# RWKV-5 attention into a cosine-routed mixture of experts: two experts named early, part of the first run as plain products

## The chip, the cores and the metric

One core of a Trainium2 chip runs the kernel. Its engines are PE (TensorE, matrix products), DVE (VectorE), ACT (ScalarE), POOL (GpSimd) and SP (SyncE, which issues DMAs here); PEld is PE's loading of weights. The metric is device time in microseconds (us), lower is better.

## The reference

```
for t in range(S):                      # B, H, S, D = 4, 8, 768, 48
    cur = einsum('bhd,bhe->bhde', u * k[t], v[t])
    y[t] = einsum('bhd,bhde->bhe', r[t], state + cur)
    state = w * state + einsum('bhd,bhe->bhde', k[t], v[t])
x = y as (B*S, H*D) = (3072, 384)
logits = (x / |x|) @ (emb / |emb|).T / tau       # 8 experts
idx = argmax(logits); gate = softmax(logits)[idx]
for e in range(8):                      # F = 1024
    h = relu(x[idx == e] @ w1[e])       # 384 -> 1024
    out[idx == e] = gate * (h @ w2[e])  # 1024 -> 384
```

## The kernel before

**Attention** runs in chunks of 64 steps, `attend` for each of 24 units (12 chunks, two units each); a unit is 128 rows of x. K, R and V are loaded chunk by chunk on SP's queue, four slots deep. ACT stores each chunk's rows to a scratch in DRAM, `xs` (L682 before, L684 after). **Routing** is done in four groups of 8, 8, 4 and 4 units (`route`): logits, the winner, its place in the expert's list by products with a triangle and with ones (L786, L787), and an addition to the list `L` (L843). It is a chain between DVE and PE.

**Settle** comes after the last group: the experts are sorted by load (`rank`, `sel`, `perm`) and `mine` takes out of `L`, for each run, the rows to gather and to write and their gates. Run i is the expert with the i-th largest load and is compiled for `CAPS[i]` rows; a row count above a cap sets a flag, and `again` does everything once more in a slow general way. `fetch` loads the weights of run i on SP (1.5 MB for w1, 1.5 MB for w2) into one of two buffers each.

**An expert** (`gather`, `expert`, `rest`): the rows of runs 0 and 1 are gathered from `xs` by POOL's indirect DMA and turned by PE (L982), those of the others by a way through DRAM and a DVE transpose. Layer one and the first 256 rows of layer two are Strassen-Winograd products with seven products for eight (L1092 and L1193); rows 256 to 383 of layer two are plain (L1170), rows from 384 on are `rest` (L1252). DVE makes the sums of w1 (L1035 to L1038), of w2 and of x (L1043 to L1046). A scatter by POOL writes the rows (L1155).

**The order** is not the program's. `Plan` records every operation with a guessed duration and its predecessors, and a list scheduler (`Plan.run`) puts out for each engine a fixed order: of the operations that can start within 0.1 us of the earliest one it takes the lowest `rank`, which is the number of the operation unless given. It also models one DMA pipe at 200 KB per us.

## Time and profile before

| | us |
|---|---|
| median of 3 runs | 451.37 (450.65 to 451.65) |
| the profiled execution | 448.21 |
| its span, first to last instruction | 446.0 |

| engine | busy us | share of the span |
|---|---|---|
| PE | 381.8 | 86% |
| PEld | 326.0 | 73% |
| DVE | 261.0 | 59% |
| POOL | 152.2 | 34% |
| ACT | 140.3 | 31% |

The busy share is a mean over three stages: attention (to about 147 us), the change-over (routing of the last group, settle, first gathers; to 182.84 us) and the experts (to the end). What the page and the trace say of each is in the rows below. Names such as `arena` are shared memory, so a line number says more than a name.

### The profile page before, as it was taken

Reading aid. Unit: us, or ns where it says so; the run is one execution under the profiler, and the core shown is the slowest. Engines: PE = TensorE matmul, PEld = TensorE weight load, DVE = VectorE, ACT = ScalarE, POOL = GpSimd, SP = SyncE. Lnnn points to the kernel's source line nnn. Section 1 sums busy time; section 2 is a strip of 40 time slices with the busy share of each in tenths; the row PEclk is TensorE's granted clock in tenths of the full one; section 3 lists DMA queues with packets and bytes.
Section 4 is the critical chain, followed back from the end, with each engine's and each line's share of the span. In section 5 each row is a group of like instructions: output and inputs, shape, how many; then the busy total and the mean of one; then the engine's idle time right before and its main releaser. Section 6 shows DMA issues by size and latency. Waiting matters only on the chain. (4 is left out here: it accounts for less than half of the span.)

```text
span 446.0 us, 11709 instructions
## 1 busy us (share of the span) xinstructions
PE 381.8 (86%) x4804; PEld 326.0 (73%) x4804; DVE 261.0 (59%) x563; ACT 140.3 (31%) x293; POOL 152.2 (34%) x188
## 2 busy tenths in 40 slices
PE   5888878988979512799999999999999999999993
PEld 3767757776758311685995896997997978979973
DVE  3885618775976388337266377377456564663521
ACT  1344523555344200032232332332141331322410
POOL 6869474866470133540160203230201201202001
PEclk8599988999898655699999999999999999999999
DMA  9766777867621169562474337346336352601001
GB/s 131 139 145 132 154 145 140 187 144 163 130 73 38 37 219 383 189 179 110 140 244 157 118 121 247 117 143 205 138 99 213 130 189 117 210 1 45 8 13 41
DMA packets 106678, 61.70 MB, mean 138 GB/s; under 512 B 87480, under 2 KB 101264, under 8 KB 106618
## 3 DMA queue, kind: packets, MB, share of 16 engines
q1 hardware_dynamic: 95770, 45.94, 38.5%
q0 software_dynamic: 3360, 9.44, 6.2%
q10 hardware_dynamic: 7488, 5.51, 4.1%
q8 instruction: 39, 0.64, 0.6%
q14 instruction: 21, 0.17, 0.1%
HBM read 48.43 MB, written 13.17 MB: 138 GB/s over the span
## 5 line engine op out<-in xcount | busy, mean ns | idle before, releaser
L1155 POOL DMA_INDIRECT out_dram<-arena,take x27 | 31.5, 1168 | 156.1 <-DVE arena L1044 70.0
L1092 PE MATMUL sc<-arena 128*128 128x192 f32 (+3 forms) x200 | 40.7, 337 | 1.1 <-ACT arena L1105 1.1
L1001 POOL DMA_INDIRECT G<-xs,take x19 | 20.6, 1086 | 54.4 <-DMA way<-G 39.9
L1092 PEld LDWEIGHTS sc<-arena 128*128 128x128 f32 x200 | 33.6, 190 | 4.2 <-ACT arena L1105 3.9
L1092 PE MATMUL yy<-arena 128*128 128x192 f32 (+3 forms) x176 | 35.4, 336 | 0.8 <-ACT arena L1105 0.6
L1116 ACT ACTIVATE arena<-arena 128x768 f32<-128x768 f32 (+3 forms) x32 | 27.5, 865 | 24.8 <-DVE arena L1109 23.9
L1092 PE MATMUL st<-arena 128*128 128x192 f32 (+3 forms) x168 | 34.5, 345 | 0.6 <-ACT arena L1105 0.6
L597 POOL TENSOR_TENSOR arena<-id,own 128x512 f32<-128x512 f32 x24 | 26.6, 1113 | 19.2 <-DVE own L593 15.9
L546 POOL TENSOR_TENSOR arena<-arena,kpow 128x384 f32<-128x384 f32 x24 | 24.6, 1024 | 21.6 <-PE tr L584 11.8
L1092 PEld LDWEIGHTS yy<-arena 128*128 128x128 f32 x176 | 29.7, 190 | 3.1 <-ACT arena L1105 2.3
L1092 PEld LDWEIGHTS st<-arena 128*128 128x128 f32 x168 | 29.6, 197 | 2.2 <-ACT arena L1105 1.6
L1092 PE MATMUL tr<-arena 128*128 128x192 f32 (+3 forms) x160 | 31.1, 331 | 0.0
L1092 PEld LDWEIGHTS tr<-arena 128*128 128x128 f32 x160 | 27.3, 190 | 0.3 <-ACT arena L1105 0.3
L1193 PE MATMUL yy<-arena 128*128 128x192 f32 x144 | 26.7, 330 | 0.9 <-ACT arena L1204 0.9
L590 POOL TENSOR_TENSOR arena<-arena,u_bc 128x384 f32<-128x384 f32 x24 | 25.0, 1044 | 6.9 <-DMA arena<-in_r_dram 6.6
L1193 PEld LDWEIGHTS yy<-arena 128*128 128x128 f32 x144 | 23.6, 190 | 2.9 <-ACT arena L1204 1.6
L1193 PE MATMUL st<-arena 128*128 128x192 f32 x120 | 22.4, 329 | 0.4 <-ACT arena L1204 0.4
L660 PE MATMUL st<-arena 64*64 64x48 f32 x704 | 18.1, 240 | 5.3 <-DMA arena<-in_v_dram 3.3
L660 PEld LDWEIGHTS st<-arena 64*64 64x64 f32 x704 | 15.0, 152 | 9.8 <-issue 4.3
L576 DVE TENSOR_TENSOR arena<-tr,pow 128x512 f32<-128x512 f32 x24 | 16.4, 685 | 9.1 <-PE tr L570 6.0
L1193 PEld LDWEIGHTS st<-arena 128*128 128x128 f32 x120 | 19.7, 190 | 1.8 <-ACT arena L1204 0.8
L591 DVE TENSOR_TENSOR arena<-arena 128x384 f32<-128x384 f32 x24 | 19.3, 803 | 2.2 <-POOL arena L590 2.1
(225 smaller groups left out, 767.6 us busy)
## 6 DMA issues: line engine op xcount, KB each, us to landing
arena<-in_moe_w_dram SPq DMA_DIRECT2D x10, 1536.0 KB
arena<-in_moe_w_dram SPq DMA_DIRECT2D x18, 512.0 KB
arena<-in_k_dram SPq DMA_DIRECT2D x48, 96.0 KB
xs<-arena ACTq DMA_DIRECT2D x12, 384.0 KB
arena<-in_r_dram SPq DMA_DIRECT2D x44, 96.0 KB
arena<-in_v_dram SPq DMA_DIRECT2D x44, 96.0 KB
Gq<-way SPq DMA_DIRECT2D x73, 48.0 KB
way<-G SPq DMA_DIRECT2D x18, 192.0 KB
```

Of the source, the lines that this page charges most:

```text
L546: p.op("POOL", gp(384), lambda: G.tensor_mul(Kw.t[:, :, 0:D], Ku(), kpow.t), r=[*Ks, kpow, k.pads], w=[Kw])
L576: lambda: V.tensor_mul(four(RT.t), four(rt.t), rpow.t[:, :, None, :].to_broadcast([128, NP, 2, C])),
L590: p.op("POOL", gp(384), lambda: G.tensor_mul(RU.t, Ru()[:, :, 0:D], k.u_bc.t), r=[*Rs, k.u_bc], w=[RU])
L591: p.op("DVE", 0.86, lambda: V.tensor_mul(RU.t, RU.t, Ku()), r=Ks, w=[RU])
L597: lambda: G.tensor_mul(AT.t, k.id64.t[:, None, None, :].to_broadcast([128, 2, NP, C]), own.t.rearrange("q (p s) -> q s p", s=2)[:, :, :, N ...
L660: mm(st.t[s * DP : (s + 1) * DP, b, (g * NP + q) * D : (g * NP + q + 1) * D], Kw.t[side(x), 2 * q + s, :], Vu()[side(x), 2 * q + s], start ...
L1001: lambda rows=rows, j=j: G.indirect_dma_start(out=rows.t[:, :], out_offset=None, in_=k.xs[:, :], in_offset=IndirectOffsetOnAxis(ap=k.take. ...
L1092: mm(bank.t[:, s * hn : (s + 1) * hn], left(2 * g + s), right(), start=(first and s == 0 and m == 0), stop=False, skip_group_check=True,)
L1116: lambda: A.activation(hT.t[:, 4 * a + 2 * g : 4 * a + 2 * g + 2, 0:n], hT.t[:, 4 * a + 2 * g : 4 * a + 2 * g + 2, 0:n], ACT.Relu),
L1155: now = G.indirect_dma_start(out=k.out[:, :], out_offset=IndirectOffsetOnAxis(ap=k.take.t[0:tn, i, 1, j : j + 1], axis=0), in_=y.t[0:tn, : ...
L1193: mm(bank.t[:, 0:192], left(s), right(s), start=(first and s == 0), stop=False, skip_group_check=True)
```

## The change

- `choose`, after the second routing group (16 of 24 units): the two experts with most rows so far are named (`two`, `perm2`), and the list of the first 256 rows of the fuller one is taken out (`take_e`, `gate_e`). `fetch` for runs 0 and 1 is recorded behind units 17 and 19 and reads `perm2`.
- `plainly`: those 256 rows (`EARLY`) go through both layers as plain products, relu and gate on ACT, with a rank of 20000 and more, so behind all else that can go; only their gathers keep a usual rank. After settle the remaining 176 rows of run 0's cap (432 - 256) go the same way, with rank 30000 and more. Run 0 has no Strassen products any more.
- `settle` does `mine` for runs 1 and 0 first; the others are sorted with a bonus that keeps the two named ones in front.
- `CAPS` goes from 432, 416, 400, 384 to 432, 416, 416, 400 for runs 0 to 3; the rest stay at 384.
- Routing operations behind the first three of a group get 60, 30, 40 and 0 added to their rank (`LATER`), except the two that free the PSUM bank.
- The shared memory of the experts is laid out anew.

```diff
+LATER = (60, 30, 40, 0)
-CAPS = (432, 416, 400, 384, 384, 384, 384, 384)
+CAPS = (432, 416, 416, 400, 384, 384, 384, 384)
+EARLY = 256
...
-        o.rank = len(self.ops) if rank is None else rank
+        o.rank = len(self.ops) + self.base if rank is None else rank
...
+    p.base = LATER[n]
     best = small("best", full)
...
+def choose(k):
...
+    def heaviest(i):
+        V.reduce_max(top.t[:, i : i + 1], so_far.t, axis=AX.X)
+        V.tensor_scalar(k.two.t[:, i], so_far.t, top.t[:, i : i + 1], None, ALU.is_equal)
...
+    p.op("DVE", 0.2, lambda: V.tensor_copy(k.perm2.t, permf.t), r=[permf], w=[k.perm2])
...
+    p.op("DVE", 0.25, lambda: V.reduce_sum(got.t, prod.t, axis=AX.X), r=[prod], w=[got])
+    p.op("DVE", 0.2, lambda: V.tensor_scalar_add(k.take_e.t, got.t[:, 1:3], float(SKIP)), r=[got], w=[k.take_e])
...
 def settle(k):
+    for i in (1, 0):
+        mine(k, i)
...
-    for i in range(E):
+    for i in range(2, E):
         mine(k, i)
...
+def plainly(k, weights, count, rows_of, gate, take, where, after):
...
+    for j, (t0, tn) in enumerate(parts(count)):
+        rows = Val(k.G, "G")
+        base, p.base = p.base, 0
+        p.op(
+            "POOL", 1.3,
+            lambda rows=rows, j=j: G.indirect_dma_start(
+                out=rows.t[:, :], out_offset=None, in_=k.xs[0:rows_of, :],
+                in_offset=IndirectOffsetOnAxis(ap=where(j, 0), axis=0),
+                bounds_check=rows_of - 1, oob_is_err=False,
+            ),
+            r=[take], w=[rows], done=2.5, kb=192, after=after,
+        )
+        p.base = base
...
+        p.op("PE", 0.36, turn, r=[rows, k.ident], w=[ps], mode=128)
...
+    for f in range(NF):
+        ps = Val(k.tre, "he")
+        def one(ps=ps, f=f):
+            for m in range(NK):
+                mm(
+                    ps.t[:, 0:count], w1.t[:, m, f * 128 : (f + 1) * 128], xT.t[:, m, 0:count],
+                    start=(m == 0), stop=(m == NK - 1),
+                )
+        p.op("PE", 3 * count * 0.00167, one, r=[w1, xT, *xs], w=[ps], mode=128)
...
+    for j, (t0, tn) in enumerate(parts(count)):
...
+        p.op("PE", 8 * 0.644 / q + 0.1, two, r=[w2, hT, *hs], w=[ps], mode=z)
...
+                if u_ + 1 == ends[1]:
+                    choose(n)
+                if u_ == 17:
+                    weights = [fetch(n, 0)]
+                if u_ == 19:
+                    weights.append(fetch(n, 1))
...
+            p.base = 20000
+            plainly(
+                n, weights[0], EARLY, 128 * ends[1], lambda j, tn: n.gate_e.t[0:tn, j : j + 1], n.take_e,
+                lambda j, a: n.take_e.t[:, a, j : j + 1], [n.stored],
+            )
+            p.base = 0
             settle(n)
-            weights = [fetch(n, i) for i in range(2)]
-            rows = [gather(n, 0)]
-            for i in range(E):
+            rows = [None, gather(n, 1)]
+            p.base = 30000
+            plainly(
+                n, weights.pop(0), CAPS[0] - EARLY, N, lambda j, tn: n.gate.t[0:tn, 0, EARLY // 128 + j : EARLY // 128 + j + 1],
+                n.takes[0], lambda j, a: n.take.t[:, 0, a, EARLY // 128 + j : EARLY // 128 + j + 1], [n.xsv.last],
+            )
+            rows.pop(0)
+            p.base = 40000
+            weights.append(fetch(n, 2))
+            for i in range(1, E):
```

**Place 1, PE, from the last routing group to the first expert.** Before: the list (L835), the total load (L856), then the turning of gathered rows (L982, buffers `G`) up to the first Strassen products.

```order
L835 MATMUL tr_69<-put_89,lanes_87 128x96 x4
L856 MATMUL tr_68<-pre_84,ones 128x8
L982 MATMUL st<-ident,G_93 128x128 x3
L1293 TENSOR_LOAD flag
L982 MATMUL st<-ident,G_94 128x128 x3
L982 MATMUL sc<-ident,G_95 128x128 x3
L982 MATMUL sc<-ident,G_96 128x48 x3
L982 MATMUL yy<-ident,G_93 128x128 x3
L982 MATMUL yy<-ident,G_94 128x128 x3
L982 MATMUL tr_69<-ident,G_95 128x128 x3
L982 MATMUL tr_68<-ident,G_96 128x32 x3
L1092 MATMUL st<-arena 128x216 x8
```

After: the total load is L937; L1352 turns gathered rows of `plainly`, L1371 is its layer one (eight groups of three), L1391 its layer two, L1064 turns the rows of run 1; the first five rows are:

```order
L937 MATMUL tr_69<-pre_84,ones 128x8
L1352 MATMUL tr_68<-ident,G_94 128x128 x3
L1371 MATMUL tr_69<-arena 128x256 x3
L1371 MATMUL tr_68<-arena 128x256 x3
L1371 MATMUL tr_69<-arena 128x256 x3
```

The products of the early rows stand behind the total load; after the sixth group of L1371, come:

```order
L1064 MATMUL st<-ident,G_95 128x128 x3
L1371 MATMUL tr_69<-arena 128x256 x3
L1064 MATMUL st<-ident,G_96 128x128 x3
L1371 MATMUL tr_68<-arena 128x256 x3
L1064 MATMUL sc<-ident,G_93 128x128 x3
L1064 MATMUL sc<-ident,G_94 128x32 x3
L1391 MATMUL tr_69<-arena 128x384 x8
L1467 TENSOR_LOAD flag
L1391 MATMUL tr_68<-arena 128x384 x8
```

The turning of run 1's rows stands between the groups of the early layer one, ahead of the early layer two.

**Place 2, ACT, the last stores to `xs`.** Before: the last store (L682) stands directly behind the copy of the last unit's result (L651).

```order
L700 COPY arena<-tr_68 128x384
L651 COPY arena<-yy 128x2x4x48
L682 DMA xs<-arena 128x2x384
L690 ACTIVATE arena,ssq<-arena 128x384
L700 COPY arena<-tr_69 128x384
L720 COPY ls_78<-tr_68 128x128
L791 ACTIVATE d_173<-d_173 128x32
L1293 TENSOR_LOAD flag
```

After: the copies of the units are L653, the squares L692, the exponential of the last routing group L794, the copies of turned early rows L1361, their relu L1380.

```order
L653 COPY arena<-yy 128x2x4x48
L692 ACTIVATE arena,ssq<-arena 128x384
L702 COPY arena<-tr_68 128x384
L722 COPY ls_78<-tr_69 128x128
L794 ACTIVATE d_184<-d_184 128x32
L684 DMA xs<-arena 128x2x384
L1361 COPY arena<-tr_68 128x3x128
L684 DMA xs<-arena 128x2x384
L1380 ACTIVATE arena<-tr_69 128x256
L1380 ACTIVATE arena<-tr_68 128x256
```

The last two stores (L684) now stand behind the exponential, and the last one behind the copy of the second early tile.

**Place 3, DVE, from the end of settle to the first copy of turned rows.** Before: the last reciprocal of `mine` (L921), the load check (L1282 to L1289), then the first copy (L991) ahead of the sums of w1.

```order
L921 RECIPROCAL gate<-gate 128x4
L1282 TENSOR_TENSOR loads<-sel,load 128x64
L1283 TENSOR_REDUCE sorted<-loads 128x8
L1285 TENSOR_SCALAR sorted<-sorted 128x1 x8
L1286 TENSOR_REDUCE over<-sorted 128x1
L1287 TENSOR_TENSOR over<-over,far 1x1
L1288 CAST flag<-over 1x1
L1289 CAST flag<-far 1x1
L991 COPY arena<-st 128x3x128
L1035 TENSOR_TENSOR arena<-arena 128x512
L1036 TENSOR_TENSOR arena<-arena 128x512
```

After: the last reciprocal of `mine` is L1003, the sums of w1 are L1119 and L1120 (L1117 and L1118 stand ahead of settle), those of w2 L1125 to L1128, the first copy of turned rows L1073.

```order
L1003 RECIPROCAL gate<-gate 128x4
L1119 TENSOR_TENSOR arena<-arena 128x512
L1120 TENSOR_TENSOR arena<-arena 128x512
L1125 TENSOR_TENSOR arena<-arena 128x768
L1126 TENSOR_TENSOR arena<-arena 128x768
L1127 TENSOR_TENSOR arena<-arena 128x768
L1128 TENSOR_TENSOR arena<-arena 128x768
L1073 COPY arena<-st 128x3x128
L1456 TENSOR_TENSOR loads<-sel,load 128x64
L1457 TENSOR_REDUCE sorted<-loads 128x8
```

The sums of w2 now stand ahead of the first copy.

## Rows read from the trace of the kernel before

**Rows 1.** The page's part 2: PE and its clock in 40 slices.

```profile
PE   5888878988979512799999999999999999999993
...
PEclk8599988999898655699999999999999999999999
```

**Rows 2.** Windows: busy PE, PEld, DVE, ACT, POOL; PEclk, DMA share, GB/s.

```profile
150.00:183.00 33.00, 9.37 (x40) 7.37 (x39) 24.73 (x97) 0.23 (x1) 10.79 (x10) 0.50 0.67 241
```

**Rows 3.** Timeline of PE in the change-over: start us, us, instruction [wait].

```profile
146.54 0.55 PE L696 MATMUL tr<-ident,arena 128*128 128x128 f32 x3 [0.60 <-ACT arena L651]
...
156.33 0.49 PE L856 MATMUL tr<-pre,ones 128*128 128x8 f32 x2
...
166.04 0.90 PE L982 MATMUL st<-ident,G 128*128 128x128 f32 x3 [9.22 <-DMA G<-xs,take]
...
182.84 3.92 PE L1092 MATMUL st<-arena 128*128 128x216 f32 x12
```

**Rows 4.** Timeline of PE, runs 0 to 4; last, an ACT copy (lines view).

```profile
188.20 1.62 PE L1092 MATMUL sc<-arena 128*128 128x216 f32 x8
...
189.69 1.00 PE L1092 MATMUL st<-arena 128*128 128x216 f32 x4
...
203.79 1.45 PE L1170 MATMUL st<-arena 128*128 128x384 f32 x4
...
209.68 2.79 PE L1252 MATMUL sc<-arena 128*48 128x384 f32 x16
...
212.39 1.57 PE L1193 MATMUL st<-arena 128*128 128x192 f32 x8
...
238.50 1.45 PE L1170 MATMUL tr<-arena 128*128 128x384 f32 x4
...
271.62 1.45 PE L1170 MATMUL tr<-arena 128*128 128x384 f32 x4
...
303.72 1.45 PE L1170 MATMUL st<-arena 128*128 128x384 f32 x4
...
333.46 1.45 PE L1170 MATMUL st<-arena 128*128 128x384 f32 x4
...
L700 ACT COPY arena<-tr 128x384 f32<-128x384 f32 x24 | 11.4, 477 | 9.4 <-PE tr L696 9.4
```

**Rows 5.** Windows as in group 2, finer.

```profile
130.00:135.00 5.00, 3.28 (x74) 2.51 (x75) 4.60 (x16) 1.31 (x4) 3.05 (x4) 0.96 0.00 0
...
135.00:140.00 5.00, 4.93 (x96) 4.34 (x91) 3.71 (x8) 2.15 (x5) 0.17 (x1) 0.70 0.01 3
...
184.00:186.00 2.00, 2.00 (x7) 1.88 (x7) 0.00 (x0) 0.00 (x0) 1.00 (x1) 0.54 0.40 144
```

**Rows 6.** Timeline of DVE between attention and the first expert.

```profile
156.58 0.25 DVE L843 TENSOR_TENSOR L<-L,tr 128x96 f32<-128x96 f32 x1 [2.12 <-PE tr L835]
...
166.42 0.18 DVE L921 RECIPROCAL gate<-gate 128x4 f32<-128x4 f32 x1
...
170.54 0.68 DVE L1038 TENSOR_TENSOR arena<-arena 128x512 f32<-128x512 f32 x1
...
175.26 0.95 DVE L1046 TENSOR_TENSOR arena<-arena 128x768 f32<-128x768 f32 x1
```

**Rows 7.** ACT's last store to xs; DMA tenths, 140 to 160 us.

```profile
146.52 0.38 ACTq L682 DMA_DIRECT2D xs<-arena  x1
...
DMA  0893100000000119910000000000000000000000
```

**Rows 8.** Gathers L971 and their landing; landing of the later ones, L1001.

```profile
L971 POOL DMA_INDIRECT G<-xs,take x8: 997/1006/1475, 159.5 to 178.0; - x8
...
DMA to landing us min/median/max: 4.3/6.0/6.8
...
DMA to landing us min/median/max: 3.0/5.9/7.4
```

**Rows 9.** Waits of PE, 45 to 147 us: total, times, longest.

```profile
PE tr L786 <- DVE oh L771: 2.8, 3, 1.1
```

More of the change, by code (lines that the diff above doesn't have):

```diff
@@ L852, in settle @@
     sb = lambda name, shape, dt=F32: p.fixed(k.sb(shape, name, dt), name)
+    k.take = sb("take", [128, E, 2, COLS], I32)
+    k.gate = sb("gate", [128, E, COLS])
+    k.got = sb("got", [128, E, 3, COLS])
+    k.gots = [p.fixed(None) for _ in range(E)]
+    k.takes = [p.fixed(None) for _ in range(E)]
+    k.gates = [p.fixed(None) for _ in range(E)]
     ct = Val(k.trr, "ct")
@@ L863, in settle @@
     )
+    for i in (1, 0):
+        mine(k, i)
+    ladj = sb("ladj", [128, E])
+    p.op(
+        "DVE", 0.21,
+        lambda: V.scalar_tensor_tensor(ladj.t, k.bonus.t, 65536.0, load_.t, ALU.mult, ALU.add), r=[k.bonus, load_], w=[ladj],
+    )
     gt = sb("gt", [128, E, E])
@@ L868, in settle @@
         lambda: V.tensor_tensor(
[L869 removed]
+            gt.t, ladj.t[:, None, :].to_broadcast(sq), ladj.t[:, :, None].to_broadcast(sq), ALU.is_gt
         ),
[L871 removed]
+        r=[ladj], w=[gt],
     )
@@ L892, in settle @@
     k.load = load_
-    k.take = sb("take", [128, E, 2, COLS], I32)
-    k.gate = sb("gate", [128, E, COLS])
-    k.got = sb("got", [128, E, 3, COLS])
-    k.gots = [p.fixed(None) for _ in range(E)]
-    k.takes = [p.fixed(None) for _ in range(E)]
-    k.gates = [p.fixed(None) for _ in range(E)]
-    for i in range(E):
+    for i in range(2, E):
         mine(k, i)
@@ L1153, in scatter @@
     def scatter(y, j, tn):
-        def put():
-            now = G.indirect_dma_start(
-                out=k.out[:, :], out_offset=IndirectOffsetOnAxis(ap=k.take.t[0:tn, i, 1, j : j + 1], axis=0),
-                in_=y.t[0:tn, :], in_offset=None, bounds_check=N - 1, oob_is_err=False,
-            )
-            for before in k.scatters:
-                k.tc.declare_no_dep(now.ins, before.ins, reason="each row of the output is in one list once")
-            k.scatters.append(now)
-        p.op("POOL", 1.3, put, r=[y, k.takes[i]], done=2.0, kb=192)
+        send(k, y, k.takes[i], lambda: k.take.t[0:tn, i, 1, j : j + 1], tn)
     gate = lambda j, tn=128: k.gate.t[0:tn, i, j : j + 1]
@@ L1236, in expert, with send, put @@
     blocks()
+def send(k, y, take, where, tn):
+    G = k.nc.gpsimd
+    def put():
+        now = G.indirect_dma_start(
+            out=k.out[:, :], out_offset=IndirectOffsetOnAxis(ap=where(), axis=0),
+            in_=y.t[0:tn, :], in_offset=None, bounds_check=N - 1, oob_is_err=False,
+        )
+        for before in k.scatters:
+            k.tc.declare_no_dep(now.ins, before.ins, reason="each row of the output is in one list once")
+        k.scatters.append(now)
+    k.plan.op("POOL", 1.3, put, r=[y, take], done=2.0, kb=192)
@@ L1470 @@
         cell = [object() for _ in range(10)]
-        n.tr, n.trx, n.trr = (p.pool(tr, [(cell[0],), (cell[1],)]) for _ in range(3))
+        n.tr, n.trx, n.trr, n.tre = (p.pool(tr, [(cell[0],), (cell[1],)]) for _ in range(4))
         n.Y = p.pool([sc, yy], [(cell[2], cell[3]), (cell[4], cell[5])])
```

128 lines of the change are left out of this document (117 added, 11 removed).

## The prediction

> **What bounds the kernel now.** I read the page's slices first. PE is at 9 in every slice from the eighteenth on and mostly at 8 in attention, but slices 14 to 17 read 5, 1, 2, 7, with PE's clock at 5 and 6 [rows 1]. Three stages then: attention, bound by PE and its partners together; a change-over in which PE has little to do; the experts, bound by PE. The windows give the hole its size: of the 33 us from 150 to 183, PE is busy 9.4, at half clock, while DVE is busy 24.7 and the DMA engines move 241 GB/s [rows 2]. The timeline says what fills it: the last product of a unit starts at 146.54, the total load ends at 156.82, the first gathered row is turned only at 166.04 after a wait of 9.22 us for its gather, and the first expert product starts at 182.84 [rows 3]. So about 26 us behind the total load are a wait for lists, gathers, 6.3 MB of weights and sums on DVE, and PE could do other work in them if it had rows and weights.
>
> **The sum** is made at one mark that both programs have: the start of the plain layer two products of run 1, at 238.50 [rows 4], L1243 in the changed kernel. Behind it the order is of the same kind; only the caps differ.
>
> Start. In the new order the early products stand directly behind the total load. I take its end as 156.82 here too (attention, below). Then come three turns of the second early tile, 0.90 at half clock [rows 3], its copy by ACT, 0.48 [rows 4], and two handoffs, 0.2 each as an estimate: layer one starts at 158.6.
>
> PE work from there. Four products of 216 columns take 189.69 - 188.20 = 1.49 us, so 1.72 ns a column [rows 4]. Early layer one: 24 x 256 columns, 10.6. Early layer two, two sets of the eight products that take 209.68 - 203.79 less a wait of 0.37, 5.5 each: 11.0. Late layer one: 24 x 176 columns, 7.3. Late layer two: one such set and 48 rows like L1252's, 212.39 - 209.68 = 2.7: 8.2. Layer one of run 1: from 212.39 to 238.50 are 26.1, of which 28 products of 192 columns take 9.2, leaving 16.9 with its own waits. Six tiles to turn, 0.45 each at full clock: 2.4, a little less for the narrow ones. Together 56.4.
>
> Losses. First the clock: from 182.84 on the products ran at 1.2 GHz, and the window from 184 to 186 still reads 0.54 [rows 5], so the rise came 3 us after the start; the same again costs 1.5. Second, a wait that the change adds. The turning of run 1's second tile writes the bank pair of the first and waits for DVE to copy it (L1073), and DVE now has the sums of w2 ahead of that copy. Behind the list at 156.58, settle took until 166.60 [rows 6]; with one operation more it ends at 166.8; two sums of w1 at 0.7 and four of w2 at 0.9 [rows 6] and the copy at 0.5 bring it to 172.2. PE gets there after six groups, one turning and a seventh: 158.6 + 1.5 + 7.9 + 0.45 + 1.3 = 169.8. Wait 2.4, and 0.6 more at the fourth tile, whose copies stand behind the load check: 3.0. In the queue behind it stands all the rest of PE's work. Third, the clock may fall in that wait: after the routing waits of the window from 130 to 135 it fell, and 135 to 140 reads 0.70 at 4.93 busy [rows 5], which is 3 us at half clock, 1.5 lost. From 0 to 1.5, I take 0.7. Fourth, the flag load that now stands between the early layer two sets, and the relu behind each layer's end: 0.4 each as at L1170, 0.8. Together 6.0, bounds 2.5 to 9.
>
> The mark falls at 158.6 + 56.4 + 6.0 = 221.0, which is 17.5 earlier.
>
> Caps. From mark to mark of the next runs are 33.1, 32.1 and 29.7 [rows 4], for caps 416 then 400, 400 then 384, 384 and 384. Runs 2 and 3 now have 416 and 400, so 33.7 (44 x 8 columns more), 33.1 and 32.1: 4.0 more. From the products alone it would be 2.6; I take 4.0, since the rows hold the handoffs too.
>
> Attention. Added to it are 16 small operations on DVE in `choose` at about 0.2 (the kind of L921) [rows 6] and two gathers on POOL at 1.0 to 1.5 [rows 8]; the next units' squares, masks and products with u queue behind them: up to 5. Taken away are routing chains ahead of unit work: PE waits 2.8 for the winner (L786) [rows 9], and 1.5 goes to the clock that falls there [rows 5]: up to 4. Both sides are of a size; I take 0, with -4 and +5 for the range.
>
> Transfers. The 6.3 MB go from the change-over to the stretch behind the last loads, where the DMA share is 0.00 and 0.01 [rows 5]: nothing, as long as the names are there. They hang on the second routing group, two groups ahead of the total load. If they came so late that w1 of run 1 landed behind 154, its first two sums (L1117, L1118), which stand ahead of the list's addition on DVE, would hold settle and the gathers by as much. The stores to xs are moved the other way. Before, the last was issued at 146.52 and its bytes moved until 149 [rows 7]; now it stands on ACT behind the copy of the second early tile, so at 158.5, and run 1's gathers cannot start before 161.5, against 159.5 before. The first lands 3.0 to 6.8 after its issue [rows 8], by 164.5 to 168.3, and PE wants it at 168.0: hidden by a hair. Here the Trainium skill speaks against the change: "DMA: Bandwidth & Descriptors", section "Issuing engines are not separate DMA queues", says that transfers from all issuing engines share the same DMA engines and interleave, so moved weights would slow what they meet. The landing times agree, 6.0 in the middle beside the weights and 3.0 at best [rows 8]; by it an early gather lands 3 us later, which changes no term, since the second early tile is turned only behind the total load.
>
> Sum: -17.5 + 4.0 + 0 = **-13.5**, so a span of 432.5. The profiled execution took 448.21, of which 446.0 is the span; it would take 434.7. The median of the runs shown, 451.37, is 3.2 above it, so 437.9.
>
> **Rivals.** *A slide*: attention or settle gets longer by 4 to 11 us, because `choose` holds DVE and POOL in units 17 to 23, or the rows of run 1 land late. For it: POOL and DVE are in order and their new rows stand amid unit work. Against it: DVE is busy 4.6 and PE 3.3 of 5 us in 130 to 135 [rows 5], so there is room. Centre +6: 444. *More*: the routing waits go (-4), DVE's copies come in time (-3.7 with the clock): 430. For it: the planner has the same chains in view. Against it: the sums stand ahead of the copy in the order. *Slower*: PE's clock stays at 1.2 GHz through the early products, which have pauses for two PSUM banks and for DVE. Its place is 158 to 182, its price 21.6 more less the 1.5 counted, so +20: -13.5 + 20 = +6.6, 458. It decides from the point where 15 us of the early work, counted at full clock, run at half. For it: all of 150 to 183 reads 0.50 although PE turned eight tiles there [rows 2]. Against it: once products came back to back at 182.84, it rose in 3 us [rows 3, 5]. The skill's "TensorE: Matmul & The Clock Gate", section "A second HAM failure mode: psum-queue depth-cycling", tells of a kernel whose short idle times between groups, as it goes round the PSUM banks, make the clock swing; by that rule 458 could come, but the Strassen groups also go round the banks, and the clock stays at 9 there [rows 1]. *It does not do what it says*: the second name may be wrong. On these inputs (counted from the reference) the two fullest experts have 272 and 271 rows after 16 units and 427 and 408 in the end, so they stay the fullest, by one row in their order; were they swapped, 427 would exceed the cap of 416, and `again` would add some thousand us.
>
> **How the numbers follow.** The forecast has 0.71, with a range of its own of 432 to 443.5 (losses and attention off by some 4 together). The slide has 0.14, of which 0.11 still ends faster and 0.03 within 0.2%; more gain 0.10; the clock 0.04, the wrong name 0.01. A measurement of this kernel can tell about 0.2% from no change, 0.9 us. Faster 0.71 + 0.11 + 0.10 = 0.92, same 0.03, slower 0.05. The range leaves out the slower cases, the worse half of the slide and the better part of more gain: 430.5 to 445.
>
> **What would show it.** In the changed profile: weights moving at 125 to 150 and the DMA share falling in 160 to 180; PE at 9 from about 158 on; PE's clock at 1.00 from about 162; a wait of PE at L1064 for DVE's L1073 near 170, some 3 us; the mark L1243 near 221; the three steps behind it 33.7, 33.1 and 32.1. The prediction is wrong if the last unit ends more than 4 us off 147, if PE waits for a gather at L1064, if L1117 waits for weights, or if the steps between the marks are those of before.

## The result, and the profile after

The changed kernel takes **457.77 us** (median of 4 runs, 456.82 to 458.70) beside 451.51 for the kernel before in the same measurement (median of 4, 450.65 to 458.28): a ratio of **1.0145**, 95% interval 1.0115 to 1.0175. Every ratio here leaves out executions more than 1.5% above the fastest of their kernel, and no median does; without the 458.28 the kernel before has 451.37, so the change costs 6.4 us. The forecast was 437.9, range 430.5 to 445.0. The profiled execution took 456.82, its span is 455.0.

The page's slices of the changed kernel (PE, its clock, the DMA engines; 11.4 us each), against [rows 1]:

```profile
PE   5886989799797958899969999999999999999894
PEclk8698897889887669899969999999999999999998
DMA  9775776876649512243373383264336352701001
```

The hole of slices 14 to 17 (5, 1, 2, 7 before) is largely filled, with 9, 5, 8 and 8, as forecast. But PE's clock is now at 6 and 7 in slices 13 to 15, where attention still runs, and there is a new dent at slice 21. Cut at the marks of the sum, between the two profiles (two single executions, 9.0 us apart in their spans where the medians are 6.4 apart):

| | before | forecast | after | off |
|---|---|---|---|---|
| total load ends | 156.8 | 156.8 | 168.1 | +11.3 |
| from there to the mark (run 1's plain layer two) | 81.7 | 64.2 | 72.8 | +8.6 |
| mark to the end | 207.5 | 211.5 | 214.1 | +2.6 |
| span | 446.0 | 432.5 | 455.0 | +22.5 |

So the gain of 17.5 that was to come between total load and mark came by half, and twice as much was lost elsewhere. One of the forecast's own signs of being wrong came up: unit 23, the last, ends 12 us later than before, not within 4.

**What came as forecast.** PE's timeline behind the total load (start us, us, instruction, the wait before it in brackets; xN counts matmul records, of which one product leaves two and a turn one), answering to [rows 3]:

```profile
167.59 0.49 PE L937 MATMUL tr<-pre,ones 128*128 128x8 f32 x2
168.15 0.90 PE L1352 MATMUL tr<-ident,G 128*128 128x128 f32 x3
169.62 9.48 PE L1371 MATMUL tr<-arena 128*128 128x256 f32 x36 [0.57 <-ACT arena L1361]
...
179.26 1.46 PE L1371 MATMUL tr<-arena 128*128 128x256 f32 x6
183.31 0.90 PE L1064 MATMUL st<-ident,G 128*128 128x128 f32 x3 [2.59 <-DVE arena L1073]
184.00 2.56 PE L1371 MATMUL tr<-arena 128*128 128x256 f32 x6
...
187.54 0.37 PE L1064 MATMUL sc<-ident,G 32*128 32x32 f32 x3 [0.65 <-DVE arena L1073]
```

Layer one of the early rows starts 1.5 us behind the total load (forecast 1.8), PE waits 2.59 and 0.65 for DVE's copies (2.4 and 0.6), six records behind the first wait take 2.56 instead of the 1.46 ahead of it (the granted clock is 0.50 from 182.8 to 186.2), and no gather is waited for.

**What did not.** Further on, PE, then DVE, then SP:

```profile
225.39 1.57 PE L1174 MATMUL yy<-arena 128*128 128x208 f32 x8
231.22 1.75 PE L1174 MATMUL sc<-arena 128*128 128x208 f32 x4 [4.27 <-ACT arena L1187]
...
240.89 1.45 PE L1243 MATMUL tr<-arena 128*128 128x384 f32 x4
```

```profile
221.75 0.59 DVE L1191 TENSOR_TENSOR arena<-yy,arena 128x416 f32<-128x416 f32 x1 [0.57 <-ACT arena L1187]
229.09 0.28 DVE L1106 STREAM_TRANSPOSE arena<-Gq 128x96 f32<-128x96 f32 x1 [6.76 <-DMA Gq<-way]
229.29 0.55 DVE L1191 TENSOR_TENSOR arena<-st,arena 128x416 f32<-128x416 f32 x1
```

```profile
208.32 2.44 SPq L1025 DMA_DIRECT2D arena<-in_moe_w_dram  x3
210.81 17.66 SPq L1099 DMA_DIRECT2D Gq<-way  x5
```

To be read from the last fence up. SP issues w1 of run 2 (L1025, three transfers of 512 KB) at 208.32, when run 0's last layer-one product, one of the late rows (L1371 with 176 columns, which end at 208.9), has freed its buffer; behind it in the queue stand 48 KB, the 32-row tile of run 2 (Gq). They land at 229. DVE has that tile's transpose (L1106) between two additions that PE's run-1 products need, so it stands 6.76 us; ACT stands behind DVE; PE stands 4.27 at 231.22. The windows add the rate and the clock (busy PE, PEld, DVE, ACT, POOL; PEclk, DMA share, GB/s):

```profile
224.00:229.00 5.00, 2.96 (x17) 2.63 (x15) 0.00 (x0) 0.00 (x0) 0.00 (x0) 1.00 0.26 96
231.00:240.00 9.00, 8.18 (x22) 6.94 (x23) 3.11 (x7) 2.49 (x5) 2.54 (x3) 0.50 0.81 266
```

While w1 moves, the DMA engines are busy 0.26 at 96 GB/s; and behind PE's wait the granted clock is 0.50 for nine microseconds: four records of 208 columns take 1.75 where eight took 1.57 before it. The wait (4.3) and nine microseconds at half clock (an estimated 4.5 lost) together make about the 8.6.

### The profile page after: what moved, and what is told of

Read it like the earlier page. It is cut to its first block, busy times and chain, and to the rows that moved or that the text cites. A ratio compares the mean times of both kernels' runs of the same rounds, so it can differ in the third digit from the quotient of the medians.

```text
span 455.0 us, 11725 instructions
## 1 busy us (share of the span) xinstructions
PE 400.1 (88%) x4806; PEld 335.6 (74%) x4806; DVE 244.8 (54%) x546; ACT 140.6 (31%) x303; POOL 152.1 (33%) x190
## 5 line engine op out<-in xcount | busy, mean ns | idle before, releaser
L1174 PE MATMUL st<-arena 128*128 128x192 f32 (+2 forms) x180 | 37.0, 337 | 1.1 <-ACT arena L1187 1.1
L1174 PE MATMUL sc<-arena 128*128 128x192 f32 (+2 forms) x144 | 31.0, 355 | 5.8 <-ACT arena L1187 4.9
L1174 PEld LDWEIGHTS st<-arena 128*128 128x128 f32 x180 | 30.2, 190 | 4.5 <-ACT arena L1187 3.6
L1174 PE MATMUL yy<-arena 128*128 128x192 f32 (+2 forms) x160 | 31.8, 335 | 1.5 <-ACT arena L1187 1.2
L1198 ACT ACTIVATE arena<-arena 128x768 f32<-128x768 f32 (+2 forms) x28 | 23.9, 862 | 28.9 <-DVE arena L1191 28.9
L1174 PEld LDWEIGHTS sc<-arena 128*128 128x128 f32 x144 | 25.8, 201 | 8.1 <-ACT arena L1187 6.5
L1174 PEld LDWEIGHTS yy<-arena 128*128 128x128 f32 x160 | 27.0, 190 | 2.8 <-ACT arena L1187 2.0
L1174 PE MATMUL tr<-arena 128*128 128x192 f32 (+2 forms) x132 | 27.4, 349 | 0.0
L592 POOL TENSOR_TENSOR arena<-arena,u_bc 128x384 f32<-128x384 f32 x24 | 24.3, 1017 | 5.5 <-DMA arena<-in_r_dram 5.4
L1266 PE MATMUL sc<-arena 128*128 128x192 f32 x136 | 25.2, 330 | 0.9 <-ACT arena L1277 0.9
L1106 DVE STREAM_TRANSPOSE arena<-Gq 128x384 f32<-128x384 f32 (+1 forms) x20 | 10.5, 536 | 27.6 <-DMA Gq<-way 17.8
L1266 PEld LDWEIGHTS sc<-arena 128*128 128x128 f32 x136 | 22.3, 190 | 2.9 <-ACT arena L1277 1.8
L1371 PE MATMUL tr<-arena 128*128 128x256 f32 (+1 forms) x96 | 20.8, 379 | 0.6 <-ACT arena L1361 0.6
```

The costliest lines, as they stand in the source:

```text
L592: p.op("POOL", gp(384), lambda: G.tensor_mul(RU.t, Ru()[:, :, 0:D], k.u_bc.t), r=[*Rs, k.u_bc], w=[RU])
L1106: lambda out=out, t0=t0, nb=nb: V.transpose(xT.t[:, :, t0 : t0 + 32 * nb].rearrange("q m (b t) -> q b m t", t=32), out.t[:, 0:nb].rearrang ...
L1174: mm(bank.t[:, s * hn : (s + 1) * hn], left(2 * g + s), right(), start=(first and s == 0 and m == 0), stop=False, skip_group_check=True,)
L1198: lambda: A.activation(hT.t[:, 4 * a + 2 * g : 4 * a + 2 * g + 2, 0:n], hT.t[:, 4 * a + 2 * g : 4 * a + 2 * g + 2, 0:n], ACT.Relu),
L1266: mm(bank.t[:, 0:192], left(s), right(s), start=(first and s == 0), stop=False, skip_group_check=True)
L1371: mm(ps.t[:, 0:count], w1.t[:, m, f * 128 : (f + 1) * 128], xT.t[:, m, 0:count], start=(m == 0), stop=(m == NK - 1),)
```

## The experiments

All times are medians, all ratios are to the kernel before, run beside them, with the 95% interval. One table for all, from the profiles: the start of the total load, from it to the mark, from the mark to the end, and attention from unit 16's output copy to unit 23's.

| kernel | us | ratio | total load | to the mark | to the end | u16 to u23 |
|---|---|---|---|---|---|---|
| before | 451.5 | | 156.3 | 82.2 | 207.5 | 39.6 |
| after | 457.77 | 1.0145 | 167.6 | 73.3 | 214.1 | 45.3 |
| e1_rank0 | 455.33 | 1.0055 (1.0006 to 1.0103) | 162.7 | 70.4 | 215.3 | 43.4 |
| e2_rank_only | 453.00 | 0.9981 (0.9923 to 1.0040) | 157.1 | 82.2 | 207.5 | 38.2 |
| e3_rows_first | 458.92 | 1.0185 (1.0076 to 1.0295) | 164.4 | 63.5 | 227.3 | 43.6 |
| e4_late_weights | 470.50 | 1.0427 (1.0337 to 1.0517) | 167.3 | 82.9 | 217.0 | 42.2 |
| e5_w1_by_rows | 448.67 | 0.9928 (0.9890 to 0.9967) | 169.7 | 63.7 | 214.1 | 45.5 |
| e6_plan_rate | 456.76 | 1.0115 (1.0068 to 1.0162) | 165.7 | 65.0 | 221.1 | 42.8 |
| e7_choose_late | 464.48 | 1.0279 (1.0196 to 1.0363) | 163.7 | 84.7 | 214.2 | 38.3 |
| e8_gathers_late | 455.94 | 1.0086 (1.0043 to 1.0128) | 168.3 | 65.9 | 220.9 | 43.2 |
| f1_rows_rank0 | 441.35 | 0.9787 (0.9718 to 0.9856) | 163.6 | 61.0 | 214.1 | 43.2 |
| f1_again | 443.18 | 0.9842 (0.9761 to 0.9923) | 166.2 | 60.2 | 214.0 | 43.2 |
| f2_choose_low | 444.65 | 0.9840 (0.9797 to 0.9883) | 169.2 | 61.3 | 214.5 | 44.2 |
| f3_old_caps | 447.05 | 0.9912 (0.9871 to 0.9954) | 167.4 | 65.1 | 212.4 | 44.1 |
| b5_w1_by_rows | 451.73 | 1.0010 (0.9963 to 1.0056) | 160.0 | 82.9 | 207.3 | 37.6 |
| g1_one_early | 435.42 | 0.9588 (0.9464 to 0.9712) | 163.1 | 57.0 | 214.3 | 43.1 |
| g2_slow_early | 440.22 | 0.9785 (0.9725 to 0.9845) | 162.4 | 61.4 | 214.1 | 40.6 |
| f4_rows_rank0_caps | 439.42 | 0.9777 (0.9722 to 0.9831) | 161.4 | 60.0 | 212.4 | 41.8 |
| h1_caps_one_early | 431.34 | 0.9533 (0.9480 to 0.9586) | 159.2 | 57.1 | 212.7 | 39.4 |

### Behind the total load: the order of the queue, or the rate of w1

e3 records run 2's fetch behind its gather, so that the 48 KB go first:

```diff
-            weights.append(fetch(n, 2))
             for i in range(1, E):
                 if i + 1 < E:
                     rows.append(gather(n, i + 1))
+                    if i == 1:
+                        weights.append(fetch(n, 2))
```

> The changed kernel with the fetch of run 2's weights recorded behind run 2's gather, so that SP issues the small transfer of the 32-row tile (Gq) ahead of the 1.5 MB of w1, which stay as late as they were. Theory: DVE's wait of 6.76 us at L1106 (229.09) is gone, PE's wait of 4.27 at 231.22 with it, and the half clock that follows from 231 to 240 (4 us); from the total load to the mark 64 to 66 us instead of 72.8, the time 449 to 451. Rival: the wait goes to the next thing that needs w1 of run 2 (its sums, L1117, on DVE ahead of PE's work), and the time falls by less than 2 us.

Up to the mark the theory came true: total load to mark is 63.5, as the sum had it. The time did not follow (458.92): the end comes 227.3 behind the mark instead of 214.1. The rival had seen that the wait would move, but not where to: it is not the sums of w1 that PE now waits for. The next tiles, those of run 3, come late, since SP needs until 221.2 for four issues that stand behind w1 of run 2. PE, there and once more a run later:

```profile
240.57 2.72 PE L1266 MATMUL st<-arena 128*128 128x192 f32 x8 [3.81 <-ACT arena L1435]
...
318.15 2.93 PE L1266 MATMUL st<-arena 128*128 128x192 f32 x8 [4.83 <-ACT arena L1277]
```

and DVE, ahead of the sums that the first of these products waits for through ACT (ahead of the second it stands 5.83 at the same line):

```profile
237.91 0.58 DVE L1106 STREAM_TRANSPOSE arena<-Gq 128x384 f32<-128x384 f32 x1 [4.17 <-DMA Gq<-way]
```

e6 leaves the transfers and tells the planner that w1 is slow:

```diff
-    p.op("SP", 0.9 if i < PLAIN else 1.4, one, ..., kb=1573)
+    p.op("SP", 0.9 if i < PLAIN else 1.4, one, ..., kb=1573 if i < PLAIN else 3146)
```

> The changed kernel with w1 of runs 2 to 7 told to the planner at twice its size (3146 kB), so that it reckons with some 100 GB/s; the transfers themselves are unchanged. In the order the transpose of the 32-row tile of run 2 now stands six of DVE's products further back. Theory (DVE's order was planned with a rate that the transfer does not have): DVE's wait before L1106 falls from 6.76 to under 3 and PE's 4.27 at L1174 goes, load to mark 64 to 68, the time 450 to 454. Rival (the rate itself, whatever the order): the wait moves by a few operations, load to mark stays above 70 or a later step grows by as much, the time 455 to 460.

The rival came true: 65.0 to the mark, but 221.1 behind it (PE waits 3.5 for one of DVE's sums, L1126, ahead of run 5's mark), and 456.76, 1.0 us below the changed kernel. Moving the wait does not pay for it.

e5 changes the transfer's form and nothing in the order of PE, DVE, ACT and POOL:

```diff
-        for c in range(NK):
-            nc.sync.dma_start(out=w1.t[:, c],
-                in_=mine_.rearrange("o (a c p) f -> c a p (o f)", a=4, p=32)[c])
+        for q in range(4):
+            nc.sync.dma_start(out=w1.t[q * 32 : (q + 1) * 32],
+                in_=mine_.rearrange("o (a c p) f -> a p c (o f)", a=4, p=32)[q])
```

> The changed kernel with w1 of runs 2 to 7 fetched in four transfers of 32 partitions (384 KB each) in place of three whose outermost dimension is 4; every engine's order is otherwise that of the changed kernel. Theory, the transfer rate of w1: in the changed kernel the DMA share reads 0.22 to 0.25 at some 100 GB/s while these weights move (212 to 229), as if four of 16 DMA engines worked; so w1 takes 15 to 17 us, the small transfers of the gathered rows queue behind it on SP, DVE waits for them in its order, and PE behind DVE. With all 16 at work the share rises to 0.8 and more, w1 lands in 5 us, DVE's wait of 6.76 at L1106 falls below 1, load to mark 63 to 66 instead of 72.8, and the wait does not come back in later steps: the time 446 to 450. Rival, the order of SP's queue itself (pools of way and Gq, DVE's order): the rate may rise, but waits of 4 us and more stay at L1106 and the time within 2 us of 457.8.

As the theory had it: 9.1 us less than the changed kernel, 63.7 to the mark, and nothing given back behind it. The window while w1 moves, and DVE at the transpose that had stood 6.76 us:

```profile
212.00:216.00 4.00, 4.00 (x15) 2.02 (x15) 0.00 (x0) 0.57 (x1) 0.00 (x0) 1.00 1.03 221
```

```profile
222.40 0.59 DVE L1191 TENSOR_TENSOR arena<-yy,arena 128x416 f32<-128x416 f32 x1 [0.57 <-ACT arena L1187]
222.90 0.27 DVE L1106 STREAM_TRANSPOSE arena<-Gq 128x96 f32<-128x96 f32 x1
```

The rate is 221 GB/s at a share of 1.03 (a packet counts with all its time in the window in which it starts, so 1 can be passed), not 96 at 0.26; PE is never late. That the same edit is worth nothing in the kernel before was to be shown too (the edit there concerns runs 2 to 7):

> The kernel before with w1 of runs 1 to 7 in four transfers of 32 partitions in place of three (run 1's form is left where it was), nothing else. Theory: before the change the slow transfer lay hidden (DVE waits 3.06 us for the 32-row tile while PE has layer two of run 0 before it), so the time stays within 0.3% of before. Rival: the rate costs the kernel before too, in its steps or in the change-over: 3 us and more faster.

Ratio 1.0010: the slow transfer lay hidden before, and the change laid it bare.

### Attention: ranks, weights, choose, gathers, or chance

```diff
-LATER = (60, 30, 40, 0)
+LATER = (0, 0, 0, 0)                    # e1; e2 adds the ranks alone to the kernel before
```

> The changed kernel with the routing's ranks put back to what they were (LATER all 0); names, early weights and early product stay. Theory A, the lower ranks of the routing made attention longer: the total load, at 168.08 in the changed kernel and 156.82 before, comes back to 156 to 160, and the time falls by 8 to 12 us, to 446 to 450. Rival B, the early names, gathers and weights made it longer: the total load stays at 165 to 170 and the time within 2 us of 457.8. The stall behind the 32-row tile of run 2 is expected in both, since its transposes still stand behind w1 of run 2.

> The kernel before with the lower ranks of the routing and nothing else. Theory A (the ranks alone lengthen attention): the total load comes 8 to 12 us later than 156.82, at 165 to 169, and the time rises to 459 to 463. Rival B: the total load within 3 us of 156.8, the time within 3 us of 451.4.

The ranks alone cost the kernel before nothing that can be measured (0.9981), as the rival had it. Without them the changed kernel is 0.9% better and its total load comes at 162.7, between the two expectations. Its profile says little of its median: 450.27 is the fastest of its ten executions, and 2.9 us of the gain lie between total load and mark. e4, e7 and e8 let the other parts of the change go out of attention, one by one, by writing the names (e4), all of `choose` (e7) or only the lists of the early rows (e8) behind the last unit:

```diff
-    p.op("DVE", 0.2, lambda: V.tensor_copy(k.perm2.t, permf.t), r=[permf], w=[k.perm2])
+    k.name = lambda: p.op("DVE", 0.2, lambda: V.tensor_copy(k.perm2.t, permf.t), r=[permf], w=[k.perm2], after=[p.ops[-1]])
...
+                if u_ == 23:
+                    n.name()
+                    weights = [fetch(n, 0), fetch(n, 1)]
```

> The changed kernel with the two names written only behind the last unit, so that 6.3 MB of weights move after attention as before and not in it; the routing's ranks, choose and the early gathers stay. Theory B1, the weights' transfers slow the loads of attention: the total load falls from 168.08 to 157 to 162; the early product then waits for w1 to about 165 to 170, and the time is within 4 us of 457.8. Theory A (ranks) and theory B2 (choose on DVE and POOL): the total load stays at 165 to 169, and the time rises by 0 to 6 us, since the early products wait for weights.

> The changed kernel with all of choose, the early gathers and the early weights behind the last unit of attention; of the change only the routing's ranks are left in attention. The early product then waits for its weights, so the time is not the question (465 to 475). Read is attention from unit 16's output copy to unit 23's: 45.3 us in the changed kernel, 42.2 with late weights alone, 38.2 with the ranks alone and 39.6 before. Theory, choose and its gathers hold DVE and POOL: 38 to 40. Rival, chance in the execution: 43 to 46.

> The changed kernel with the lists of the early rows (take_e) written behind the last unit, so that the two early gathers leave POOL's order in attention; choose and the early weights stay. Theory, the gathers hold POOL (3.30 us idle for gate_e at 133.56 in the changed kernel, and units queue behind them): unit 16 to unit 23 falls from 45.3 to 39 to 41, the total load comes 4 to 6 us earlier. Rival, choose on DVE or the weights' transfers: 43 to 46. The gathers then land about 5 us behind the lists, which themselves come about with the total load: the early product starts some 3 to 6 us later, the time 452 to 460 in either case.

(e8 names both experts in time; PE waits 3.9 for its late gathers and more behind the mark, 220.9.)

By the total load, as it was written, e4 rejects the weights: 167.3; its time, 470.50, is above both expectations, since the early product waits for its weights. That measure was a bad one. Up to unit 16 the changed kernel, e2 to e8 and f3 have the same order, and yet unit 16's copy comes anywhere from 109.3 to 116.0; in the stretch behind it, e4 is down by 3.1, e8 by 2.1, e7 by 7.0 to 38.3, the level of e2 (38.2). So late weights take away 3.1, and taking `choose` and its gathers out as well another 3.9, in one profile each. The last four units, from unit 19's copy to unit 23's, say it best. The changed kernel:

```profile
135.06:158.13 23.07, 20.20 (x460) 17.38 (x458) 13.26 (x31) 8.67 (x22) 10.34 (x11) 0.70 0.82 305
```

and e2:

```profile
129.73:147.49 17.76, 14.96 (x461) 12.51 (x461) 11.85 (x30) 8.90 (x23) 6.50 (x8) 1.00 0.13 48
```

The same 460 records take 20.20 us at a mean clock of 0.70 and 14.96 at 1.00. Over all profiles this stretch takes 17.8 to 20.1 where no weights move in it (before, b5, e2, e7, e4) and 21.5 to 24.9 where the 6.3 MB do (twelve). In eleven of these twelve one wait of PE stands in it. In the changed kernel, the second profile of f1, and e4, which has the changed kernel's order there but no weights:

```profile
142.20 0.58 PE L627 MATMUL yy<-arena 48*64 48x64 f32 x10 [1.87 <-issue]
```

```profile
141.40 0.47 PE L642 MATMUL sc<-arena 64*64 64x48 f32 x9 [2.36 <-issue]
```

```profile
142.97 0.74 PE L627 MATMUL yy<-arena 48*64 48x64 f32 x32
```

"Issue" is a wait whose end no semaphore explains; what ends it is in the last section. It stands at different lines, but at the same count of PE's matmul records (the windows up to the wait, changed kernel and f1_again):

```profile
0.00:142.00 142.00, 116.06 (x3141) 96.74 (x3142) 88.28 (x182) 57.81 (x140) 88.84 (x130) 0.87 0.72 148
```

```profile
0.00:141.30 141.30, 112.04 (x3142) 93.91 (x3143) 90.54 (x181) 57.23 (x137) 90.33 (x131) 0.93 0.74 149
```

Of the fourteen profiles with early weights in this stretch, thirteen have it there with 1.9 to 2.65 us; of the five without early weights none has it. f2 is the exception, and a warning: it has no such wait there, its order of routing and units is its own, PE waits 3.37 for ACT (L589) instead, and the stretch still takes 24.3. In the thirteen the mean clock of the stretch is 0.68 to 0.92, and 1.00 in h1; in the five it is 0.91 to 1.00.

f1 puts the ranks back on top of e5, f2 also ranks `choose` 100 lower, g1 on top of f1 lets only run 0's weights move in attention (run 1's name is written behind the last unit), and g2 was to slow w1 of runs 0 and 1 down:

> The changed kernel with w1 in four transfers (as in e5_w1_by_rows, 448.67) and the routing's ranks put back. Theory, the lower ranks cost the first 16 units some 4 us: the profiles with them have unit 16's output copy at 109 to 116, those without at 106 and 110; here 107 to 111, and the time 443 to 446. Rival, the ranks cost nothing that lasts (with the ranks alone the kernel before ran in 453.0 against 452.3): the time 447 to 450.

> f1_rows_rank0 once more, unchanged, beside the three others and with a second profile. 441.35 (440.69 to 442.59) is to come again within 2 us. Its second profile tells what chance does to attention: if the stretch from unit 8 to unit 16 (41.4 in the first) comes at 45 or more, the ranks have no part in it, as in the kernel before with the new form of w1 (45.2).

> As f1_rows_rank0, and the operations of choose ranked 100 lower, so that unit work which is ready goes ahead of them. Theory, choose costs by standing in DVE's and PE's order ahead of units: unit 16 to unit 23 falls from 43 to 46 to 39 to 42 (38.3 with choose behind attention), and the time is 2 to 5 us below f1_rows_rank0. Rival, it costs by what it starts (weights and gathers) or the names come too late: no gain, or a loss of up to 4 us.

```diff
+    k.name = lambda: p.op("DVE", 0.2, lambda: V.tensor_copy(k.perm1.t, permf.t), r=[permf], w=[k.perm1], after=[p.ops[-1]])
...
-                if u_ == 19:
+                if u_ == 23:
+                    n.name()
                     weights.append(fetch(n, 1))
```

> As f1_rows_rank0 (441.35), with the name of run 1 written only behind the last unit, so that run 0's weights (3.1 MB) move in attention and run 1's 3.1 MB behind it. Theory, the transfer in attention costs PE there: where weights move, unit 19 to unit 23 takes 22.6 to 24.9 us and PE stands 1.9 to 2.6 us at one instruction with no wait that the trace shows, where none moves 17.8 to 20.1; with half the bytes 19 to 22, and the time 437 to 441. Rival, not the transfer but choose and its gathers lengthen these units: 22.5 and more. The planner now also puts some early products between the last routing steps, which may be worth 2 us more.

```diff
-            nc.sync.dma_start(out=w1.t, in_=mine_.rearrange("o (c p) f -> p (o c) f", p=128))
+            nc.sync.dma_start(out=w1.t, in_=mine_.rearrange("o (c a p) f -> a p (o c) f", a=4, p=32))
```

> As f1_rows_rank0, with w1 of runs 0 and 1 fetched in a form whose outermost dimension is 4, so that it goes by a quarter of the DMA engines at some 100 GB/s; same bytes, same order on every engine. Theory, it is the full load on the DMA engines that keeps something else waiting (300 GB/s and a share of 0.8 in units 19 to 23): at 0.3 to 0.4 the unexplained wait of 2 us is gone, unit 19 to unit 23 takes 18 to 21 instead of 22.9; w1 of run 1 then lands near 166 and holds the lists by 2 to 5 us, mostly beside the early product: the time 437 to 442. Rival, the bytes and not their rate: 22 to 25, and the time 441 to 446.

f1 is better than its theory had it (441.35; 443.18 in f1_again is inside), but only partly for the reason named. From e5 it has 2.7 less to the mark: in its order the tiles of run 1 are turned behind all 48 records of the early layer one, so the two waits for L1073 are gone. The rest lies in attention, where f1_again weakens the theory of the ranks: unit 8 to unit 16 takes 44.7 in it and 41.4 in the first, with one program, just short of the 45 that was to settle it. f2 gains nothing, so ranking `choose` lower does not help. g2 told nothing on the rate: the transfer stayed as fast as it was (329 GB/s from unit 19 to 23), presumably because the dimensions of this form can be joined, and its 440.22 is a third f1. g1 is 6 to 8 us better than the two f1, but not as forecast: unit 19 to 23 still takes 23.06, with 2.3 at the same record. Its gain is behind the total load, 57.0 to the mark, because layer one of the early rows now runs between the last routing steps, as h1's timeline also has it:

```profile
151.55 1.56 PE L1373 MATMUL tr<-arena 128*128 128x256 f32 x6
152.95 0.27 PE L740 MATMUL tr<-ident,ls 128*128 128x128 f32 x1
153.59 1.56 PE L1373 MATMUL tr<-arena 128*128 128x256 f32 x6 [0.36 <-ACT arena L1382]
154.99 0.30 PE L789 MATMUL tr<-oh,umask 128*128 128x32 f32 x2
155.13 0.39 PE L790 MATMUL tr<-pre,ones 128*128 128x32 f32 x2
155.62 2.86 PE L1373 MATMUL tr<-arena 128*128 128x256 f32 x12
158.32 1.03 PE L840 MATMUL tr<-put,lanes 128*128 128x96 f32 x8
```

### The caps, and the best of it

`CAPS` as before in e5 (f3), in f1 (f4) and in g1 (h1):

> e5_w1_by_rows with the caps of before (432, 416, 400, 384, ...), which hold on these inputs. It prices the wider caps: forecast was 4.0 us for three steps between the marks; in the changed kernel these take 35.8, 34.0 and 31.3 where they took 33.1, 32.1 and 29.7, so 6.1. Theory, the whole of it is the caps: the three steps come back to 94 to 96 in sum, the time to 442 to 445. Rival, part of it is the new place in the order (waits behind ACT and DVE): the sum stays at 97 to 99, the time 445 to 447.

> f1_rows_rank0 with the caps of before. By f3_old_caps against e5_w1_by_rows (447.05 against 448.67) the wider caps cost 1.6 us: 439 to 441. By the steps between the marks (4.0 forecast): 436 to 438.

> g1_one_early with the caps of before. g1 ran in 435.42; the caps were worth 1.6 us (f3 against e5) and 3.8 us (f4 against f1_again), so 431 to 434 by either. Theory that g1's gain is the early start of layer one between the routing's last steps: total load to mark 57 again, as in g1, where f1_rows_rank0 has 61.

From mark to end the old caps give 212.4, 212.4 and 212.7 for 214.1, 214.1 and 214.3: the wider ones cost 1.6 to 1.7 us there. f3's three steps between the marks take 99.2, where the changed kernel has 101.1 and the kernel before 95.0: its rival, that part of it is the new order, came true. h1 beats both kernels: 431.34 us, 0.9533 of the kernel before (0.9480 to 0.9586). Between the profiles of g1 and h1 part of the difference is luck (g1's took 436.38, its four executions run from 428.96 to 437.28), and that part is instructive: g1 and h1 have one order in attention and the same wait of PE in it (2.31 and 1.99), but in g1 the clock fell behind it and in h1 it did not. Unit 19 to 23 in g1:

```profile
130.01:153.07 23.06, 19.34 (x461) 16.15 (x462) 13.21 (x31) 8.87 (x22) 9.47 (x11) 0.78 0.48 171
```

and in h1:

```profile
129.63:149.11 19.48, 15.38 (x461) 12.68 (x462) 13.21 (x31) 8.66 (x22) 9.47 (x11) 1.00 0.56 203
```

So the wait itself, beside the 17.8 of e2, costs some 2 us, and the clock 3.6 more.

## Why the prediction was wrong

**What bounds the kernel, the early product, the losses: right.** The hole was where the rows had it, and PE could fill it. With the transfer mended (e5), total load to mark is 63.7 from the start of the load and 63.2 from its end, beside 64.2 in the sum. The waits for L1073 were placed and sized rightly (2.59 and 0.65 in the changed kernel; 1.38 and 0.65 in e5).

**Transfers, "nothing": wrong, +8.6.** The step asked when the early weights move and whether a gather is late. It did not ask of w1 of run 2, whose form and place behind run 0 the change leaves as they were. Before, its buffer was free and SP issued it at 197.5, 41 us ahead of the mark:

```profile
197.51 7.00 SPq L943 DMA_DIRECT2D arena<-in_moe_w_dram  x3
```

Now the plain products of run 0 hold it until 40 us behind the total load, 24 ahead of where the sum has the mark. All that stands behind it on SP's queue moved with it, and DVE's order holds a transpose for one of those tiles in the middle of run 1. The rate could have been read in the trace of before: from 204 to 212, behind that issue, the DMA share is 0.26.

```profile
204.00:212.00 8.00, 7.63 (x32) 3.53 (x30) 7.68 (x17) 1.09 (x2) 0.77 (x1) 1.00 0.26 104
```

The Trainium skill states it too, and the forecast overlooked it: "DMA: Bandwidth & Descriptors", section "Why a DMA increments its semaphore by 16 and not by 1", says that a transfer uses the largest number of engines up to 16 that divides the slowest dimension of both sides. By that rule the outermost 4 gives 4 of 16 engines, a share of 0.25; the trace has 0.26, and 1.03 with an outermost dimension of 32. e5 (rate) against e3 and e6 (order) shows the cause: with the rate mended the stall is gone for good, with the order mended alone it comes back in a later run.

**Attention, "0, -4 to +5": wrong, +11.3, in three pieces.** From unit 16 to 23 it is 5.7 between the two profiles. The forecast had named DVE and POOL under `choose` as the risk. What they cost stays open: ranking `choose` lower (f2) gains nothing and late lists (e8) 2.1, but from e4 to e7 3.9 go with them, in one profile each. It had taken the weights as free there, since the DMA share was 0.00 [rows 5], and had asked only of a gather what the moved weights would slow. Where they move, PE stands 1.9 to 2.65 us at one point in thirteen of fourteen profiles, and its clock mostly falls. Before unit 16 it is 6.4, and there the greater part is chance: with the ranks of before, unit 16's copy comes at 106.4 to 114.4 in ten profiles (mean 111.0), with the lower ranks at 109.3 to 116.0 in nine (mean 113.6), and the profile that the forecast was built on is the earliest of all. Some 2.6 may be the ranks (the standard error of that difference is 1.0); e2's time did not show them. The routing of the last group gives 0.9 back. The forecast's correction of 3.2 from the profile to the median was right for the kernel before, but it put no width on it.

**Caps, +4.0: mis-sized, and a term was missing.** The caps cost 1.7, less than the forecast's sum of products alone (2.6). The other 4.9 of the 6.6 behind the mark stay with the caps of before (f3, f4, h1: 212.4 to 212.7 against 207.3 to 207.5). The forecast had put nothing on waits of the new order there. PE's windows from the mark to its last product, the kernel before and f3:

```profile
238.50:440.00 201.50, 196.95 (x1065) 170.53 (x1064) 114.98 (x230) 59.02 (x108) 31.82 (x27) 1.00 0.36 121
```

```profile
232.53:439.33 206.80, 197.97 (x1065) 170.51 (x1064) 114.90 (x230) 58.56 (x108) 33.73 (x30) 1.00 0.46 124
```

With the same number of records PE is idle 8.8 us in f3 and 4.6 before, and busy 1.0 longer; that is the 4.9, but for a few tenths at the end. Among the waits that the kernel before had not, by the changed kernel's list from 240 us on:

```profile
PE sc L1174 <- DVE arena L1284: 1.0, 1, 1.0
...
PE st L1266 <- ACT arena L1435: 0.7, 1, 0.7
PE yy L1243 <- DVE arena L1191: 0.7, 1, 0.7
```

Which part of the change puts them there (the new place in the order, or the new layout of memory) was not tried and stays open.

**The rivals.** "Slower" landed on the measured time (458) by luck: through the early product the clock did not stay at 1.2 GHz (169 to 180 reads 0.84). "A slide" had the right sign and the wrong place. None of them had a transfer that the change leaves as it is and only makes later. With 0.92 on "faster" the chances were much too sure: they weighed only what the new code does, not what it pushes back.

## What to carry over

When work moves, follow each buffer that it holds: what is loaded into it next, what stands behind that load on its queue, and who has to wait for those in a fixed order. A DMA share near a quarter while one large transfer moves (0.26 here) is a sign to look at its outermost dimension before anything is moved against it. And read several profiles of the kernel before: a stretch that varies by 8 us between executions of one order (unit 16 at 106.4 to 114.4) can't be a fixed point of a sum made to one.

## What the runs showed of the hardware

PE's waits marked "issue" come at a fixed spacing in its own instructions. The kernel before, the window up to such a wait and the row of the wait:

```profile
0.00:108.50 108.50, 87.42 (x2507) 74.02 (x2507) 69.22 (x128) 47.14 (x113) 74.85 (x115) 0.89 0.76 148
```

```profile
108.55 0.41 PE L712 MATMUL tr<-arena,ent 128*32 128x128 f32 x3 [1.39 <-issue]
```

f1_again has 0.84 at the same 2507.

Other such waits stand at 472, 598, 1107, 1235, 1743, 1870, 2123, 2250, 2379 and 3142 matmul records: 126 to 129 apart, or a multiple of that, with one weight load each, so some 254 PE instructions. They last from 0.2 to 2.65 us, differ from one execution to the next, and the longest come while 300 to 400 GB/s move. That fits the supply of PE's instructions, and the DMA packets of the traces bear it out. The profile's queue q8 is named "instruction" and moves 39 packets of 16 KB in each execution, and 136 of the 138 such waits of PE in the nineteen profiles end 1.2 to 1.7 us behind the end of one of them. Before the wait of 1.87 in the changed kernel (the DMA view from 139.8 to 140.8: packets, MB, share):

```profile
q8 instruction: 1, 0.02, 5.8%
```

At record 3142 this packet takes 0.9 to 1.2 us in every profile, and 0.9 to 1.0 where the wait stands behind it; what differs is when it starts. In the five without early weights it starts at records 3039 to 3045, early enough to be hidden; in the thirteen with the wait at 3123 to 3142; in f2 at 3055. The windows up to it, and the four microseconds ahead of it, changed kernel and then e4:

```profile
0.00:139.80 139.80, 115.53 (x3122) 96.35 (x3123) 86.22 (x176) 57.32 (x139) 87.05 (x129) 0.87 0.72 144
135.86:139.86 4.00, 3.87 (x150) 3.19 (x144) 3.11 (x8) 2.57 (x7) 3.83 (x6) 1.00 0.99 375
```

```profile
0.00:141.05 141.05, 115.88 (x3038) 97.22 (x3042) 83.19 (x172) 56.38 (x136) 85.54 (x126) 0.88 0.69 134
137.10:141.10 4.00, 3.80 (x122) 3.04 (x123) 3.38 (x7) 2.51 (x6) 3.97 (x4) 1.00 0.46 150
```

So the late block of instructions is shown. That it is late because it stands behind the weights is argued from the share of 0.99 against 0.46; no row shows the order inside the DMA engines. The Trainium skill, "Runtime: NRT & Kernel Launch", section "Instruction fetch mechanics", tells of blocks of 256 instructions that the sequencer fetches by DMA, at a cost that is mostly hidden. Spacing and packets agree with it, and so does "mostly": up to 160 us of the changed kernel 27 blocks are fetched, and six of them end in a wait.

The second thing is what a short wait of PE can cost in clock: behind 4.27 us at 231.22 nine microseconds ran at 0.50, and in attention 3.6 us went behind a wait of 2 in one execution and nothing in another (g1, h1). A wait on PE's path is priced too low if it is priced by its length.
